# Block 2 of a fused attention and GeGLU kernel: two pairs of units in seven products, another order of units, earlier numerators and a later load of v

## The chip, the cores and the metric

The kernel runs on one core of one Trainium2 chip. The metric is the time of one execution on the device in microseconds (us). Three runs of the kernel before the change gave a median of 306.35 us (306.07 to 306.92).

## The reference

Inputs are q, k and v (batch 8, heads 8, sequence 576, head dimension 64) and three weight matrices. Attention is linear: no softmax over pairs of positions.

```python
def phi(x, c, s):                       # c, s: cosine and sine of pi/2 * position / 576
    r = np.maximum(x, 0.0)
    return np.concatenate([r * c, r * s], axis=-1)
kv = np.einsum('bhsf,bhsd->bhfd', k_p, v)        # k_p = phi(k), q_p = phi(q)
z = np.sum(k_p, axis=2)
num = np.einsum('bhsf,bhfd->bhsd', q_p, kv)
den = np.einsum('bhsf,bhf->bhs', q_p, z)[..., None] + 1e-06
x = (num / den)                          # then as 4608 tokens x 512
gelu = 0.5 * g * (1 + erf(g / sqrt(2)))  # g = x @ w_gate   (512 x 1536)
out = (gelu * (x @ w_val)) @ w_out       # 4608 x 512
```

## The kernel before

The work has two streams that are woven by hand. The attention goes by batch `b` (0 to 7, 576 tokens each). The feed-forward part goes by block `n` (0 to 8) of 512 tokens, so block 2 holds the last 128 tokens of batch 1 and 384 of batch 2, and block 3 the last 192 of batch 2 and the first 320 of batch 3. Each engine executes its instructions in the order in which the program issues them. TensorE is PE, VectorE is DVE, ScalarE is ACT, GpSimd is POOL, and SyncE (SP) issues most DMAs.

**Attention.** `load` brings q, k, v of a batch into staging (`st`, or `sm` and `fs` for some batches). The preps multiply the positive part by cosine (`c`) or sine (`s`), for one of nine groups of positions at a time; `prep_both` does q and k together, and `EARLY` lists by unit of block 2 which groups of batch 4 are prepared ("s0 c0": sine and cosine of group 0). There `early` puts sines on ACT, and cosines on POOL up to unit 8 and on ACT later. `cast_v` rounds v, `kv_unit` makes the product of k and v, and `turn_q` transposes q by two DMAs on SP. `nm_unit(b, t)` makes the numerators of 128 tokens: eight matmuls into PSUM banks 6 and 7, then on DVE a small add (`den`), a reciprocal (`rec`) and the division (`x_sb`, one of four buffers in turn, so that (3,2) takes that of (2,3) and (3,4) that of (3,0)). `turn_x(b, t)` transposes such a tile into `xT` by DMA on SP.

**Gate and value.** A unit is 128 of the 1536 columns of the gate and value weights, for one block. `gv_unit` (matmuls L431) runs four matmuls of 512 columns for the gate into one bank, a gelu on ACT (L440), four for the value into another bank, and a multiplication on DVE (L443) into the hidden tile `hT`. Block 2 of the kernel before makes all twelve units in this way, units 0 to 3 as two halves of 256 tokens each. Blocks 3 to 8 make most units two at a time, by `Pair`: seven products (`p1` to `p7`, L655) of four 256-column matmuls each stand for the eight that a plain two-by-two split needs. They need sums of weights (`ws`, `wx`), made in early blocks, and four sums of x, T1 to T4, made by `x_sum` on POOL (L635) in `fs`. Product 5 needs T1, product 6 T2, product 7 T3 and product 4 T4. Between the products ACT copies partial results (L674 copies product 1 from the pair's sum bank to its other bank, L678 product 5 to `fs`), and DVE adds (L682 after product 6, L695 after product 7) and multiplies (L696, L700). `step` writes out the order for one pair, with pieces of other work (`a`, `b`, `c`) between products. With `std` set it also makes one plain unit, with product 4 between its gate and its value.

**Output.** `o_step(n, jt)` does one or two of the fourteen products of the previous block's output (`product`, matmuls L548, six of 256 columns each, in banks 4 and 5). Copies (L566) and additions (L561) follow on ACT and DVE, and sums of hidden tiles (`h_sum`, L530) on DVE in block 2 and on POOL from block 3.

In the trace of before, block 2 runs on PE from 79 to 111 us. SP gives its DMAs eight completion semaphores in turn, so that an issue also waits for the landing of the DMA eight issues before it.

Of the kernel before, what the change touches and what calls it, by code (L numbers as in the profile page):

```python
# [10 lines left out]
BF16 = mybir.dt.bfloat16  # L11
# [5 lines left out]
def kernel(  # L17
# [20 lines left out]
    JT = J // 128  # L38
    NP = H // 2
    R = S // 64  # L40
    NB = B * S // 512
    NT = 5
    EPS = 1e-6
    BLK = 512
# [37 lines left out]
    fs = fast.tile([128, 5 * BLK], FP32)  # L82
# [138 lines left out]
    def turn_q(b):  # L221
        for i in range(2):
            nc.sync.dma_start_transpose(
                out=qt_tile(b)[:, i].rearrange("f m (j p) -> f (m j) p", p=64),
                in_=phi["q", b][64 * i:64 * i + 64].rearrange("p m j f -> p (m j f)"),
            )
# [83 lines left out]
    def nm_unit(b, t, b0=6):  # L310
        for h in range(H):
            nc.tensor.matmul(  # L312
                bank(b0 + h // 4)[:, (h % 4) * (D + 1):(h % 4 + 1) * (D + 1)],
                lhsT=q_cols(b, t, h),
                rhs=kv_sb[b][:, h // 2, h % 2, :],
                start=True,
                stop=True,
            )
        nm = ps[:, b0:b0 + 2, 0:4 * (D + 1)].rearrange("p g (h d) -> p g h d", h=4)
        den = attn2.tile([128, 2, 4], FP32, name="den")  # L320
        rec = attn2.tile([128, 2, 4], FP32, name="rec")
        x = xsp.tile([128, 2, 4, D], BF16, name="x_sb")
        nc.vector.tensor_scalar_add(den, nm[:, :, :, D], EPS)
        nc.vector.reciprocal(rec, den)
        nc.vector.tensor_tensor(  # L325
            x,
            nm[:, :, :, 0:D],
            rec[:, :, :, None].to_broadcast([128, 2, 4, D]),
            op=ALU.mult,
        )  # L330
        xs[b, t] = x.rearrange("p g h d -> p (g h d)")
# [44 lines left out]
    def turn_x(b, t):  # L376
        x = xs.pop((b, t))
        for blk, c, o, m in pieces(b, t):
            nc.sync.dma_start_transpose(
                out=xT_block(blk)[:, :, c:c + m], in_=x[o:o + m, :]  # L380
            )
# [13 lines left out]
    turn = [0]  # L395
# [25 lines left out]
    def gv_unit(n, jt, c0=0, w=BLK, to=None, between=None):  # L421
        xt = xT[n]
        js = slice(jt * 128, (jt + 1) * 128)
        if to is None:
            to = (0, 1) if turn[0] % 2 == 0 else (2, 3)
            turn[0] += 1
        if n not in hT:
            hT[n] = ffn.tile([128, JT, BLK], BF16, name="hT")
        for g, wt in ((0, wg_sb), (1, wv_sb)):
            for ct in range(CT):  # L430
                nc.tensor.matmul(  # L431
                    bank(to[g])[:, 0:w],
                    lhsT=wt[:, ct, js],
                    rhs=xt[:, ct, c0:c0 + w],
                    start=(ct == 0),
                    stop=(ct == CT - 1),
                )
            if g == 0:
                gel = ffn.tile([128, BLK], FP32, name="gel")
                nc.scalar.activation(gel[:, 0:w], bank(to[0])[:, 0:w], AF.Gelu)  # L440
                if between:
                    between()
        nc.vector.tensor_mul(  # L443
            hT[n][:, jt, c0:c0 + w], gel[:, 0:w], bank(to[1])[:, 0:w]
        )
# [57 lines left out]
    hs, rest = {}, [0]  # L503
# [119 lines left out]
    def x_sum(n, i, eng=nc.gpsimd):  # L623
        if n not in xb:
            xt = xT[n]
            own = fs[:, (n % 2) * 2 * BLK:(n % 2 + 1) * 2 * BLK].bitcast(BF16)
            xb[n] = {
                "B11": xt[:, 0:CP, 0:256], "B12": xt[:, 0:CP, 256:512],
                "B21": xt[:, CP:CT, 0:256], "B22": xt[:, CP:CT, 256:512],
                "T": own.rearrange("p (i c n) -> p i c n", i=4, c=CP),  # L630
            }
        b = xb[n]
        x, y = (("B12", "B11"), ("B22", "T1"), ("B22", "B12"), ("B21", "T2"))[i]
        b[f"T{i + 1}"] = b["T"][:, i]
        eng.tensor_tensor(b[f"T{i + 1}"], b[x], b[y], op=ALU.subtract)  # L635
# [98 lines left out]
    HALF = BLK // 2  # L734
# [151 lines left out]
    def js(a, b):  # L886
# [2 lines left out]
    LOADS = {  # L889
        (1, 4): [(3, "k")], (1, 9): [(3, "v", 0)], (1, 11): [(3, "v", 2)],  # L890
        (2, 0): [(4, "q", 0, 5), (4, "k", 0, 5)],
        (2, 2): [(4, "q", 5, R), (4, "k", 5, R), (4, "v")],
        (2, 9): [(5, "q", 0, 5), (5, "k", 0, 5)],
        (3, 1): [(5, "q", 5, R), (5, "k", 5, R), (5, "v")],
        (3, 9): [(6, "q", 0, 5), (6, "k", 0, 5)],
# [12 lines left out]
    MORE = {}  # L908
    for n in (3, 4, 5, 6):
        for i in range(4):  # L910
            MORE.setdefault((n - 1, 8 + i), []).append((n, i))
    for i, name in enumerate(("S1", "S3", "S2", "S4")):
        MORE.setdefault((6, i), []).append((name, WX, J))
    for i in range(4):
# [3 lines left out]
    def more(n, jt):  # L918
        for what in MORE.get((n, jt), ()):
            if len(what) == 3:  # L920
                w_sum(*what, eng=nc.gpsimd)
            else:
                x_sum(*what)
# [42 lines left out]
    def block1():  # L966
        b, n = 2, 1
        for jt in range(JT):
            i = jt - 9
            if i > 0:  # L970
                nm_unit(b, i, (4, 6, 4)[i])
                turn_x(b, i)
            if jt < 2:
                for i in range(2):
                    half, unit = divmod(2 * jt + i, 2)
                    x3 = lambda: turn_x_pe(1, 3, 5, dve_copy)
                    gv_unit(n, unit, half * HALF, HALF, between=x3 if jt == i == 0 else None)
                    j = JA + 2 * jt + i
                    prep("q", b, 1, (j,), eng=nc.scalar)
                    prep("q", b, 0, (j,))  # L980
            else:
                gv_unit(n, jt, between=(lambda: nm_unit(b, 0, 4)) if i == 0 else None)
            if i == 0:
                turn_x(b, 0)
            if jt % 3 == 1:
                flush()
            if jt == 2:
                prep("q", b, 0, (R - 1,))
                prep("q", b, 1, (R - 1,), eng=nc.scalar)
                turn_q(b)  # L990
                nm_unit(1, NT - 1)
            if jt == 5:
                turn_x(1, NT - 1)
            if jt == 6:
                kv_unit(b)
            if jt in (0, 1, 2, 7):
                wo_sum({0: "T3", 1: "T1", 2: "T2", 7: "T4"}[jt])
            if jt in SCALE:
                scale(*SCALE[jt])
            if jt in (3, 4):  # L1000
                cast_v(b, 2 * (jt - 3), 2 * (jt - 3) + 2, act_copy)
            if jt == 11:
                nm_unit(b, 3, 6)
            start_loads(n, jt)

    EARLY = {
        6: "s0 c0 s1 c1", 7: "s2 c2 s3", 8: "c3 s4", 9: "c4 s5", 10: "c5 s6", 11: "c6 s7",
        12: "c7 s8 c8",
    }

    def early(jt):
# [4 lines left out]
    def block2():  # L1016
        b, n = 3, 2
        o_step(n, 0)
        for jt in range(JT):
            if jt >= 4:  # L1020
                gv_unit(n, jt, to=(2, 6) if jt == JT - 1 else None)
            else:
                for i in range(2):
                    half, unit = divmod(2 * jt + i, 4)
                    gv_unit(n, unit, half * HALF, HALF)
                    if jt == i == 0:
                        nm_unit(2, 4)
                        turn_q(3)
            if 0 <= jt - 6 < NT:
                turn_x(b, jt - 6)  # L1030
            if 0 < jt < JT - 1:
                o_step(n, jt)
            if 0 <= jt - 5 < NT:
                nm_unit(b, jt - 5)
            if jt + JT in SCALE:
                scale(*SCALE[jt + JT])
            if jt in (1, 2):
                cast_v(b, 2 * jt - 2, 2 * jt, act_copy)
            if jt == 3:
                kv_unit(b)  # L1040
            early(jt)
            if jt == 1:
                turn_x(2, 3)
                turn_x(2, 4)
            start_loads(n, jt)
            if jt in (8, 9):
                m = 2 * (jt - 8)
                cast_v(4, m, m + 2, nc.gpsimd.tensor_copy)
            more(n, jt)

    turn[0] = 1
    block1()
    block2()

    PREPS = {
        2: "s0 c0", 4: "s1 c1", 5: "s2", "m10": "c2", 6: "s3 c3", 7: "s4 c4",
# [49 lines left out]
    def slot(n, jt):  # L1106
        o_step(*divmod(n * JT + jt - 1, JT))
        attention(n, jt)
        more(n, jt)
        if n == NB - 1 and jt in (9, 10):  # L1110
            h_sum(n, jt - 9, "S3", eng=nc.gpsimd)
        if n == NB - 1 and jt == 11:
            for name in ("S1", "S2", "S4"):
                h_sum(n, 0, name, 0, JH - 2, eng=nc.gpsimd)

    def slots(n, *jts):
        return [lambda jt=jt: slot(n, jt) for jt in jts]

    old, places = None, (0, 1, 2)
    for n in range(3, NB):  # L1120
        jt = 0
        for T in range(JT // 2):
# [3 lines left out]
            at, other, to = places  # L1126
# [60 lines left out]
```

## Time and profile before

| | |
|---|---|
| median of three runs | 306.35 us |
| the profiled execution | 305.74 us, its span 304.0 us |
| granted TensorE clock | 0.999 |
| busy, share of the span | PE 97%, DVE 75%, ACT 67%, POOL 55% |
| chain that ended last | PE 75%, DMA 8% |

PE is the row of matmuls and PEld that of weight loads, which lie beside the matmuls. In a timeline, a row gives start and duration (us), engine, line, operation, output and inputs, and how many; in brackets stands the idle time of the engine before it and what ended that. Rows of matmuls overlap their successors, since a matmul's end is counted when its last column leaves the array: what a group occupies is the distance from its start to the next group's start. In the chain of waits each row is the start, the length, and the engine or DMA that the end was waiting for at that moment.

### The profile page before, as it was taken

To read this page: it belongs to the slowest core of one execution; us is meant where nothing else is said; L and a number is where in the kernel's file an instruction comes from. 1 tells how busy PE (TensorE), PEld (TensorE's weight loads), DVE (VectorE), ACT (ScalarE), POOL (GpSimd) and SP (SyncE) were. 2 spreads that over 40 slices of the span, in tenths; PEclk is the share of its full clock that TensorE was granted. 3 is DMA by queue.
4 is the path that set the end of the run, shared out by engine and by line. 5 is a ranking of instruction groups with operands and counts; after the bars stand their busy time and mean duration, and the time that the engine had idled before them with its cause. 6 is when DMAs were issued, how large, how long until landed. Compare 5 with 4: busy or idle time off the path is not lost.

```text
span 304.0 us, 8032 instructions
## 1 busy us (share of the span) xinstructions
PE 294.7 (97%) x3089; PEld 228.8 (75%) x3107; DVE 226.7 (75%) x496; ACT 202.2 (67%) x399; POOL 165.9 (55%) x140
## 2 busy tenths in 40 slices
PE   7899999999999999999999999999999999999993
PEld 3574456745786668887888788888898988888882
DVE  5866995998986655779677967796679785766772
ACT  7865592997572787969686958694645556555630
POOL 6675450000000979976944694569935965397310
PEclk9999999999999999999999999999999999999999
DMA  7999999979999999997998899928824221303045
GB/s 269 258 174 218 338 293 390 309 162 224 183 169 231 320 239 170 207 298 215 130 238 251 215 135 226 277 31 136 139 55 71 53 51 30 71 0 73 2 87 121
DMA packets 73176, 53.68 MB, mean 177 GB/s; under 512 B 45393, under 2 KB 62545, under 8 KB 73137
## 3 DMA queue, kind: packets, MB, share of 16 engines
q1 hardware_dynamic: 63360, 41.17, 60.9%
q0 software_dynamic: 9696, 11.93, 17.1%
q8 instruction: 24, 0.39, 0.5%
q14 instruction: 16, 0.12, 0.2%
q10 hardware_dynamic: 80, 0.07, 0.1%
HBM read 37.75 MB, written 9.44 MB: 155 GB/s over the span
## 4 chain that ended last, share of the span: by engine, by line
PE 75%; DMA 8%; issue 5%; DVE 4%; POOL 3%; ACT 2%; SPq 1%; POOLq 0%; DVEq 0%; ACTq 0%
PE ps L655 32%; PE ps L548 19%; PE ps L431 14%; DMA st<-in_v_dram 5%; PE ps L464 3%; PE ps L271 3%; PE ps L312 2%; DMA wv_sb<-in_moe_w_val_dram 2%; DVE hT L443 2%; SPq L98 1%; POOL st L530 1%; DMA xT<-x_sb 1%; ACT phis L178 1%; PE ps L402 1%; POOL fs L635 1%
## 5 line engine op out<-in xcount | busy, mean ns | idle before, releaser
L530 POOL TENSOR_TENSOR sm<-hT 128x768 bf16<-128x768 bf16 x24 | 39.4, 1643 | 18.5 <-PE ps L655 8.0
L431 PE MATMUL ps<-xT,wg_sb 128*128 128x512 bf16 (+1 forms) x172 | 41.3, 349 | 0.6
L431 PE MATMUL ps<-xT,wv_sb 128*128 128x512 bf16 (+1 forms) x182 | 41.8, 351 | 0.1
L695 DVE TENSOR_TENSOR ps<-fs,ps 128x512 f32<-128x512 f32 x33 | 23.0, 696 | 24.7 <-PE ps L655 23.2
L655 PE MATMUL ps<-fs,ws 128*128 128x256 bf16 x288 | 40.8, 273 | 0.1
L655 PEld LDWEIGHTS <-ws 128*128 128x128 bf16 x384 | 36.5, 98 | 5.1 <-ACT ps L674 0.3
L655 PE MATMUL ps<-xT,wg_sb 128*128 128x256 bf16 x264 | 39.6, 272 | 0.0
L194 POOL TENSOR_SCALAR phis<-st,cos_t 128x512 bf16<-128x512 f32 x4 | 8.2, 2067 | 52.4 <-DMA st<-in_k_dram 52.4
L443 DVE TENSOR_TENSOR hT<-gel,ps 128x512 bf16<-128x512 f32 (+1 forms) x46 | 28.0, 613 | 11.5 <-PE ps L431 8.8
L548 PEld LDWEIGHTS <-sm 128*128 128x128 bf16 x336 | 32.3, 98 | 4.5
L440 ACT ACTIVATE gel<-ps 128x512 f32<-128x512 f32 (+1 forms) x46 | 24.6, 542 | 15.7 <-PE ps L431 14.5
L687 ACT ACTIVATE gel<-ps 128x512 f32<-128x512 f32 x33 | 19.6, 594 | 18.3 <-PE ps L655 18.3
L548 PEld LDWEIGHTS <-hT 128*128 128x128 bf16 x288 | 27.9, 98 | 4.0 <-issue 0.2
L561 DVE TENSOR_TENSOR o_sb<-sm,ps 128x256 f32<-128x256 f32 x56 | 23.3, 416 | 10.1 <-ACT sm L566 8.9
L678 ACT COPY fs<-ps 128x512 f32<-128x512 f32 x33 | 19.4, 587 | 16.2 <-DVE ps L695 15.3
L431 PEld LDWEIGHTS <-wv_sb 128*128 128x128 bf16 x184 | 17.9, 98 | 15.2 <-issue 0.3
L655 PEld LDWEIGHTS <-wg_sb 128*128 128x128 bf16 x264 | 25.8, 98 | 4.7
L325 DVE TENSOR_TENSOR x_sb<-ps,rec 128x512 bf16<-128x512 f32 x38 | 26.3, 691 | 1.3
L192 ACT ACTIVATE phis<-st,sin_t 128x512 bf16<-128x512 f32 x36 | 25.6, 718 | 0.0
L530 POOL TENSOR_TENSOR sm<-hT,sm 128x768 bf16<-128x768 bf16 x12 | 19.7, 1645 | 10.8 <-PE ps L548 10.8
L431 PEld LDWEIGHTS <-wg_sb 128*128 128x128 bf16 x184 | 17.0, 98 | 11.4
L696 DVE TENSOR_TENSOR hT<-gel,ps 128x512 bf16<-128x512 f32 x33 | 22.7, 687 | 3.2
(134 smaller groups left out, 636.0 us busy)
## 6 DMA issues: line engine op xcount, KB each, us to landing
out_dram<-o_sb SPq DMA_DIRECT2D x69, 128.0 KB, 3.0
st<-in_v_dram SPq DMA_DIRECT2D x10, 576.0 KB, 7.5
st<-in_q_dram SPq DMA_DIRECT2D x5, 640.0 KB, 5.4
st<-in_q_dram SPq DMA_DIRECT2D x5, 512.0 KB, 5.6
st<-in_k_dram SPq DMA_DIRECT2D x4, 640.0 KB, 5.9
st<-in_k_dram SPq DMA_DIRECT2D x4, 576.0 KB, 4.6
st<-in_q_dram POOLq DMA_DIRECT2D x4, 576.0 KB, 12.1
st<-in_k_dram SPq DMA_DIRECT2D x4, 512.0 KB, 5.4
```

The source lines that it names most:

```text
L192: nc.scalar.activation(o, i, AF.Relu, scale=tab[:, j:j + 1])
L325: nc.vector.tensor_tensor(x, nm[:, :, :, 0:D], rec[:, :, :, None].to_broadcast([128, 2, 4, D]), op=ALU.mult,)
L431: nc.tensor.matmul(bank(to[g])[:, 0:w], lhsT=wt[:, ct, js], rhs=xt[:, ct, c0:c0 + w], start=(ct == 0), stop=(ct == CT - 1),)
L440: nc.scalar.activation(gel[:, 0:w], bank(to[0])[:, 0:w], AF.Gelu)
L443: nc.vector.tensor_mul(hT[n][:, jt, c0:c0 + w], gel[:, 0:w], bank(to[1])[:, 0:w])
L530: eng.tensor_tensor(a[name][:, j0:j1], a[x][:, j0:j1], a[y][:, j0:j1], op=op)
L548: nc.tensor.matmul(at, lhsT=hs.setdefault(key, h_parts(n, p))[a][:, j], rhs=ts[b][:, j], start=(j == 0 and i in ((1, 2, 4, 5), (1, 4, 5))[ ...
L561: nc.vector.tensor_tensor(o, got[key, k], x, op=op)
L655: nc.tensor.matmul(to[:, 256 * half:256 * half + 256], lhsT=w_part(a, j * 128, (j + 1) * 128)[:, ct], rhs=xb[self.n][b][:, ct], start=(hal ...
L687: nc.scalar.activation(self.gel0, self.other, AF.Gelu)
L695: nc.vector.tensor_tensor(bank(val), self.m5, self.sum, op=ALU.add)
L696: nc.vector.tensor_tensor(self.h(1), both(gel1), both(bank(val)), op=ALU.mult)
```

## The change

Block 2 takes units 8 to 11 first, as halves, then unit 4 whole, then units 0 and 1 as a pair with unit 5 plain inside it, units 2 and 3 as a pair with unit 6 inside it, and unit 7 at the end. The sums of x for block 2 are made on POOL at unit 2, and those for blocks 2 and 3 change halves of `fs`. The work that was put behind each unit is now the function `rest`, in which the numerators of batch 3 and their transposes stand one unit sooner. All four sums for block 3 are issued at unit 8, and the casts of v of batch 4 follow them at units 9 and 10. v of batch 4 is loaded at unit 7, where it was at unit 2. The preps of batch 4 are spread differently, and the last unit uses banks 0 and 6 where it was 2 and 6.

```diff
     def x_sum(n, i, eng=nc.gpsimd):
-            own = fs[:, (n % 2) * 2 * BLK:(n % 2 + 1) * 2 * BLK].bitcast(BF16)
+            own = fs[:, (1 - n % 2) * 2 * BLK:(2 - n % 2) * 2 * BLK].bitcast(BF16)
...
-        (2, 2): [(4, "q", 5, R), (4, "k", 5, R), (4, "v")],
+        (2, 2): [(4, "q", 5, R), (4, "k", 5, R)],
+        (2, 7): [(4, "v")],
...
-            MORE.setdefault((n - 1, 8 + i), []).append((n, i))
+            MORE.setdefault((n - 1, 8 + i * (n > 3)), []).append((n, i))
...
     EARLY = {
-        6: "s0 c0 s1 c1", 7: "s2 c2 s3", 8: "c3 s4", 9: "c4 s5", 10: "c5 s6", 11: "c6 s7",
-        12: "c7 s8 c8",
+        7: "c0 c1 c2 c3 s0 s1 s2", 8: "s3 s4", 9: "c4", 10: "s5 c5 s6", 11: "c6 s7 c7",
+        12: "s8 c8",
     }
...
     def block2():
         b, n = 3, 2
         o_step(n, 0)
-        for jt in range(JT):
-            if jt >= 4:
-                gv_unit(n, jt, to=(2, 6) if jt == JT - 1 else None)
-            else:
-                for i in range(2):
-                    half, unit = divmod(2 * jt + i, 4)
-                    gv_unit(n, unit, half * HALF, HALF)
-                    if jt == i == 0:
-                        nm_unit(2, 4)
-                        turn_q(3)
-            if 0 <= jt - 6 < NT:
-                turn_x(b, jt - 6)
+
+        def rest(jt):
+            if 0 <= jt - 5 < NT:
+                turn_x(b, jt - 5)
             if 0 < jt < JT - 1:
                 o_step(n, jt)
-            if 0 <= jt - 5 < NT:
-                nm_unit(b, jt - 5)
+            if 0 <= jt - 4 < NT:
+                nm_unit(b, jt - 4)
...
             start_loads(n, jt)
-            if jt in (8, 9):
-                m = 2 * (jt - 8)
+            if jt == 2:
+                for i in range(4):
+                    x_sum(n, i)
+            more(n, jt)
+            if jt in (9, 10):
+                m = 2 * (jt - 9)
                 cast_v(4, m, m + 2, nc.gpsimd.tensor_copy)
-            more(n, jt)
+
+        def rests(*jts):
+            return [lambda jt=jt: rest(jt) for jt in jts]
+
+        turn[0] = 1
+        for jt in range(4):
+            for i in range(2):
+                half, unit = divmod(2 * jt + i, 4)
+                gv_unit(n, unit + 8, half * HALF, HALF)
+                if jt == i == 0:
+                    nm_unit(2, 4)
+                    turn_q(3)
+            rest(jt)
+        gv_unit(n, 4, to=(2, 6))
+        rest(4)
+        step(Pair(n, 0, 0, 2, range(5, 8)), None, *rests(5, 6, 7), std=5, to=1)
+        step(Pair(n, 1, 2, 0, range(8, 11)), None, *rests(8, 9, 10), std=6, to=1)
+        gv_unit(n, 7, to=(0, 6))
+        rest(11)
```

More of the change, by code (lines that the diff above doesn't have):

```diff
@@ L1045, in block2 @@
             start_loads(n, jt)
-            if jt in (8, 9):
-                m = 2 * (jt - 8)
-                cast_v(4, m, m + 2, nc.gpsimd.tensor_copy)
-            more(n, jt)
-    turn[0] = 1
-    block1()
-    block2()
+            if jt == 2:
[4 more added lines that the diff above has]
+                m = 2 * (jt - 9)
+                cast_v(4, m, m + 2, nc.gpsimd.tensor_copy)
+        def rests(*jts):
[15 more added lines that the diff above has]
+        rest(11)
     PREPS = {
@@ L1117, in slots @@
         return [lambda jt=jt: slot(n, jt) for jt in jts]
+    turn[0] = 1
+    block1()
+    block2()
     old, places = None, (0, 1, 2)
```

## The prediction

> **What bounds the kernel now.** I read the page first, then the chain of waits from 85 to 116 us, then the timelines of TensorE (PE), VectorE (DVE), ScalarE (ACT), GpSimd (POOL) and SyncE (SP) over block 2, 79 to 113 us. Page, part 1:
>
> ```profile
> PE 294.7 (97%) x3089; PEld 228.8 (75%) x3107; DVE 226.7 (75%) x496; ACT 202.2 (67%) x399; POOL 165.9 (55%) x140
> ```
>
> PE is the bound, and in block 2 its matmuls follow each other without a hole but one. So whatever PE no longer runs is gained, and every new wait of PE is lost one for one. The chain of waits (start, us, what) tells of that hole:
>
> ```profile
> 96.60 0.83 SPq L98
> 97.48 9.34 DMA st<-in_v_dram
> 106.83 2.76 DMA xT<-x_sb
> 109.61 1.15 POOL fs L635
> 110.76 1.09 POOL vx L209
> 111.86 1.12 POOL fs L635
> 113.02 1.03 PE ps L655 x8
> ```
>
> v of batch 4 lands, then the x tiles behind it, then POOL makes T1, casts, makes T2, and product 6 of block 3 starts at 113.02. The PE timeline has the hole and, earlier, unit 4 with what follows:
>
> ```profile
> 91.78 1.03 PE L431 MATMUL ps<-xT,wv_sb 128*128 128x512 bf16 x4
> 92.65 0.82 PE L548 MATMUL ps<-T,hT 128*128 128x256 bf16 x6
> 93.30 1.03 PE L431 MATMUL ps<-xT,wg_sb 128*128 128x512 bf16 x4
> 112.14 0.82 PE L548 MATMUL ps<-wo_sb,sm 128*128 128x256 bf16 x6
> 113.02 0.60 PE L655 MATMUL ps<-fs,ws 128*128 128x256 bf16 x4
> ```
>
> Six matmuls of 256 occupy PE 0.66 (92.65 to 93.30), so PE was free at 112.80 and stood 0.22. DVE and ACT, same stretch:
>
> ```profile
> 92.92 0.69 DVE L443 TENSOR_TENSOR hT<-gel,ps 128x512 bf16<-128x512 f32 x1 [1.28 <-PE ps L431]
> 107.84 0.16 DVE L323 TENSOR_SCALAR den<-ps 128x8 f32<-128x8 f32 x1
> 108.03 0.20 DVE L324 RECIPROCAL rec<-den 128x8 f32<-128x8 f32 x1
> 108.27 0.69 DVE L325 TENSOR_TENSOR x_sb<-ps,rec 128x512 bf16<-128x512 f32 x1
> 110.60 0.60 ACT L440 ACTIVATE gel<-ps 128x512 f32<-128x512 f32 x1 [0.20 <-PE ps L431]
> 111.09 0.71 ACT L192 ACTIVATE phis<-st,cos_t 128x512 bf16<-128x512 f32 x1
> 111.71 0.71 ACT L192 ACTIVATE phis<-st,sin_t 128x512 bf16<-128x512 f32 x1
> 112.32 0.58 ACT L674 COPY ps<-ps 128x512 f32<-128x512 f32 x1
> ```
>
> Each engine works in program order. ACT starts some 0.20 after PE is free, DVE 0.27 (92.65 to 92.92), PE some 0.05 after the DVE or ACT result it needs (T2 ended 112.98, PE 113.02). ACT's copy of product 1 ended 112.90, so without T2's wait product 6 still stands about 0.13 there.
>
> **The products.** A unit is eight 512-column matmuls, four in 0.865 (91.78 to 92.65): two units 3.46. A pair is seven products of four 256-column matmuls, 0.4375 each (116.57 to 117.01 in block 3): 3.06. Gain 0.40 a pair, **0.80** for two. The Trainium skill, "TensorE: Matmul & The Clock Gate", Back-to-back issue gap, speaks against that: sustained it gives about 131 ns for a 512-column matmul and 81 for 128, so, put between them (an estimate), about 98 for 256, and a pair would take 2.73 against 2.10 and two pairs cost 1.3. This trace has 216 and 109, and I go by it.
>
> **Parts that I cost at nothing.** Units 8 to 11 as halves: the same rows; hT of block 2 is read first at 113.89. Sums of block 2's x: four on POOL at 1.11 each, behind the second cast of v 3 (ACT, 88.03 to 89.17): done 93.7. POOL is idle until 98.06; the last is read by p4 at about 101; if that cover went, p5 (94.4) and p6 (95.8) would wait for T1 (90.4) and T2 (91.5), which have over 4 us to spare. DVE's sums of hidden tiles (0.55 each) would lie beside them, which no row of before shows; bounds 0 to 0.5 on DVE, I take 0, as POOL and DVE durations elsewhere (block 3) are alike with and without overlap. The Trainium skill, "GPSIMD Engine Reference", has GpSimd's SBUF interfaces shared with VectorE where a DVE instruction has two SBUF inputs; no row here overlaps the two. v of batch 4 (two issues of 0.5 to 0.8 on SP) goes behind the tiles of (3,2) and two stores; I expect landing near 109 and 110. POOL: c0 to c3 end 106.2, four x sums to 110.7, casts to 113.0. kv of batch 4 wants them at about 116.5: 3 us of cover. On SP the move takes two issues from ahead of all the tiles of batch 3: before, a tile's issue at 106.83 stood until v had landed at 106.81. Behind v on SP there are now the tiles of (3,3) and (3,4) and the first loads of batch 5, which need prep c4 (ACT, 107.7; before 108.0): no one waits for those before block 3. The single units 5 and 6 use one bank for gate and value: the gelu ends 0.80 after the gate, while PE has a product, a numerator and p4, over 1.1. New fs half: no time. Last unit into banks 0 and 6: product 1 of block 3 needs bank 0, read by the gelu that ends 0.20 + 0.60 = 0.80 after the gate; the value matmuls take 0.865. Hidden by 0.02 at worst, a wait of 0.05 otherwise.
>
> **Numerators a unit sooner: new waits of PE.** Times in the clock of before.
> (a) nm(3,0) follows unit 4 and product 4, at 93.30. It writes bank 6, where unit 4's value now lies (to=(2, 6)), and DVE reads that until 92.92 + 0.69 = 93.61. PE goes on at 93.66: **0.36**. Its other inputs are there (turned q landed 92.95 by the trace's completion updates, kv copies by 91.7).
> (b) nm(3,1), after p1, p5 and a product (0.44 + 0.44 + 0.66), wants bank 6 at 95.45. DVE runs o_sb, a hidden sum (to 94.40), den, rec and x of nm(3,0) to 95.5: **0.10**.
> (c) x(3,2) reuses the buffer of x(2,3), whose transposed tile landed at 99.98. Before, DVE wrote x(3,2) at 102.52 and saw nothing; now it would at 99.55 and stands to 100.03. Behind it on DVE: the add of product 7, which p4 waits for. x to 100.7, add to 101.35. PE: nm(3,3) **0.08** (bank 6), and p4, wanted at 101.03, **0.35**. If that tile landed 1.5 sooner, both are 0; nothing ahead of it in the queue is changed, so I take 0.43.
> (d) Second pair. nm(3,4) stands right ahead of p6. DVE after PE's end of nm: 0.27, den 0.20, rec 0.24, x 0.61, then p6's add, 0.69, and 0.05 back: 2.06. p3 overwrites the add's bank and needs it; PE has p6, p2 and one product till then, 0.44 + 0.44 + 0.66 = 1.54: **0.53**. In the first pair the same place has two products and a numerator (2.0 after p6), no wait.
> (e) p4 of the second pair: add of product 7 waits for gelu behind prep c4 on ACT: **0.05**.
>
> **ACT's preps.** Now c6, s7, c7 follow the last unit's gelu, before c6, s7: three steps of 0.62 ahead of product 1's copy. From the gate's end: 0.20 + gelu 0.49 + 1.85 + copy 0.58 + 0.04 = 3.16. PE till product 6: value 0.865, p1 and p5 0.875, product 0.66 = 2.40. Wait **0.76**, in place of 0.22; T2 (108.6) is no longer late. What follows is c8, s8: ACT had slack there (0.93 idle at 116.67).
>
> **Sum.** 0.36 + 0.10 + 0.43 + 0.53 + 0.05 + 0.76 = 2.23 of waits, less the old 0.22, less 0.80: +1.21 us. The profiled execution took 305.74 (span 304.0, 1.74 around it) and would take 306.95; it stood 0.61 under the median of the runs, 306.35. Median forecast: 306.35 + 1.2, about **307.5**, 0.4% slower. Block 3 and later are bound by PE and shift as a whole.
>
> **Rivals.**
> 1. Faster: the waits are covered and the products count. Full gain 0.80 + 0.22: 305.3. For it: PE has one hole in 35 us, and pairs in block 3 run without (a wait of 0.08 in the first). Against: there products of the pair before lie between; here (a) and the ACT row are arithmetic on in-order queues. It decides at waits under 0.1 in sum. Chance 0.07.
> 2. About even: (c) goes and DVE and ACT are 0.1 to 0.2 quicker to respond at (d) and product 6: +0.3 to +0.9, centre 306.9. Nothing against it but the rows' repeatability. Chance 0.25.
> 3. The x buffers bite: x(3,4) reuses the buffer of x(3,0). Before, that tile landed 107.99 behind v of batch 4; v took 103.26 to 106.24 of the queue, so I place it at 105.0, and DVE wants the buffer at 105.19. If moving v frees nothing, DVE stands to 108 and p3 waits 3.4 instead of 0.53: +4.1, 310.4; half of that, +2.5, 308.9. It decides from 105.2 on, one for one. Chance 0.12.
> 4. The change does not bring the x tiles sooner: T2 stays late. That lies under the 0.76 of ACT until T2 passes 114.2 (before 112.98). Cost 0; part of 3.
>
> **How the numbers follow.** Forecast case 0.56, own range 307.0 to 308.2 (bounds: (e), the 0.1 and the DVE sharing above, 0 to 0.5, each way). About 0.3% (0.92 us: 305.43 to 307.27) is what a measurement of this kernel can tell from no change. Slower by more: most of the forecast case (0.49) and case 3, 0.61. Faster: case 1 with little else, 0.07. Within: 0.32. The range 306.2 to 308.9 leaves out case 1 and the far half of case 3 and some of the rest, 0.2 in all.
>
> **What would show it.** Right: nm(3,0) starting 0.05 after DVE's L443 of unit 4; DVE's x at the third numerator ended by an xT transfer; a hole of about 0.5 before p3 of the second pair; 0.7 to 0.8 before product 6 of block 3 with ACT L674 as its releaser; and product groups of 0.44. Wrong: no holes of PE in block 2, or a hole above 1 us at p3 of the second pair (case 3), or one at kv of batch 4 (v too late), or matmul groups of the pairs longer than 0.44.

## The result, and the profile after

The changed kernel takes 307.57 us (median of 22 runs, 306.76 to 308.58), against 306.58 us for the kernel before in the same rounds (22 runs, 305.08 to 307.17). The ratio is 1.004 with a 95% interval of 1.0028 to 1.0053: slower by 0.9 to 1.6 us. All ratios here are of fast runs: two of the twelve runs of the last kernel below were slow ones, 309.95 and 310.18 us, some 4 above the other ten, for which no trace shows a cause, and they stand outside its ratio.

The profiled execution of the changed kernel took 308.40 us (span 306.6). That is 2.7 more than the profiled one of before, but part of it has nothing to do with the change: the work ahead of block 2 ended anywhere from 78.5 to 80.3 us in the profiles of this case, with the same program there. So the text compares a **stretch**: from the first output product of block 2 to the first product of k and v of batch 4, early in block 3. It is 36.27 us before (36.22 in a second execution) and 37.97 after, a loss of 1.70. From there to the last matmul both take the same, 183.25 and 183.26 us. All of the loss is in the stretch. Where an expectation reckons to product 6 of block 3, which starts 2.28 sooner, that is 33.99 before and 35.68 after.

From the page of the changed kernel (engine, busy time, share of the span, instructions):

```profile
PE 295.4 (96%) x3131; PEld 231.0 (75%) x3131; DVE 230.6 (75%) x500; ACT 203.9 (66%) x403; POOL 169.2 (55%) x144
```

PE's busy time is no lower than before and its share fell: time was lost to holes. The timeline of PE over the places that the prediction named:

```profile
93.59 0.82 PE L548 MATMUL ps<-T,hT 128*128 128x256 bf16 x6
94.60 0.42 PE L312 MATMUL ps<-kv_sb,qT 128*128 128x65 bf16 x8 [0.19 <-DVE hT L443]
...
95.73 0.82 PE L548 MATMUL ps<-wo_sb,sm 128*128 128x256 bf16 x6
97.04 0.42 PE L312 MATMUL ps<-kv_sb,qT 128*128 128x65 bf16 x8 [0.50 <-DVE x_sb L325]
97.30 0.60 PE L655 MATMUL ps<-fs,ws 128*128 128x256 bf16 x4
97.73 0.60 PE L655 MATMUL ps<-xT,wg_sb 128*128 128x256 bf16 x4
...
107.76 0.60 PE L655 MATMUL ps<-xT,ws 128*128 128x256 bf16 x4 [0.29 <-DVE ps L682]
```

Six matmuls of 256 columns occupy 0.655, so nm(3,0) stood 94.60 − 93.59 − 0.655 = 0.36 and nm(3,1) 97.04 − 95.73 − 0.655 = 0.66 (the idle time in brackets is less by some 0.16, since a matmul's end is counted later). A group of a pair takes 97.73 − 97.30 = 0.43. The timelines of DVE and of POOL ahead of nm(3,1):

```profile
91.43 0.55 DVE L530 TENSOR_TENSOR sm<-hT 128x768 bf16<-128x768 bf16 x1
92.01 1.39 DVE L530 TENSOR_TENSOR sm<-sm,hT 128x768 bf16<-128x768 bf16 x1
93.86 0.69 DVE L443 TENSOR_TENSOR hT<-gel,ps 128x512 bf16<-128x512 f32 x1 [0.45 <-PE ps L431]
...
94.80 1.16 DVE L530 TENSOR_TENSOR sm<-hT 128x768 bf16<-128x768 bf16 x1
```

```profile
91.43 1.56 POOL L635 TENSOR_TENSOR fs<-xT,fs 128x512 bf16<-128x512 bf16 x1
92.95 1.46 POOL L635 TENSOR_TENSOR fs<-xT 128x512 bf16<-128x512 bf16 x1
94.38 1.15 POOL L635 TENSOR_TENSOR fs<-xT,fs 128x512 bf16<-128x512 bf16 x1
```

Hidden sums on DVE that take 0.55 alone took 1.39 and 1.16, and two of the sums of x on POOL took 1.56 and 1.46 instead of 1.15. In order of their ends: DVE 91.98, POOL 92.99, DVE 93.40, POOL 94.41, POOL 95.53, DVE 95.96. It reads as one of them standing until the other's instruction is through.

The chain of waits at the end of the block (start, us, what), where before the x tiles and T2 stood:

```profile
113.17 1.93 ACT phis L192 x3
115.11 0.49 ACT ps L674
115.60 0.05 issue
115.65 1.05 PE ps L655 x8
```

Behind the last unit's gelu stand three preps, the copy of product 1, and product 6 at 115.65. PE had been free since 114.86, a hole of 0.79.

The holes of PE in the stretch, but for those of 0.10 that both kernels have at products of k and v. A hole is there where the distance of two matmuls is more than the first one's length (0.216 for 512 columns, 0.109 for 256, 0.033 for 65):

| hole ahead of | predicted | measured |
|---|---|---|
| (a) nm(3,0) | 0.36 | 0.36 |
| (b) nm(3,1) | 0.10 | 0.66 |
| (c) nm(3,3) and p4, first pair | 0.08 + 0.35 | 0 + 0.28 |
| (d) p3, second pair | 0.53 | 0.46 |
| (e) p4, second pair | 0.05 | 0.13 |
| first product of block 3 | 0 to 0.05 | 0.03 |
| product 6 of block 3 | 0.76 | 0.79 |
| sum | 2.23 | 2.71 |

2.71 less the old hole of 0.23 less 0.80 for the pairs is +1.68, and the stretch grew by 1.70. It is a little more than the top of the timed interval, 1.62; nothing here explains the rest.

### The profile page after: what moved, and what is told of

Its sections match the earlier page's. It is cut to its first block, busy times and chain, and to the rows that moved or that the text cites. A ratio compares the mean times of both kernels' runs of the same rounds, so it can differ in the third digit from the quotient of the medians.

```text
span 306.6 us, 8114 instructions
## 1 busy us (share of the span) xinstructions
PE 295.4 (96%) x3131; PEld 231.0 (75%) x3131; DVE 230.6 (75%) x500; ACT 203.9 (66%) x403; POOL 169.2 (55%) x144
## 4 chain that ended last, share of the span: by engine, by line
PE 78%; DVE 7%; issue 5%; DMA 5%; ACT 2%; POOL 1%; SPq 0%; POOLq 0%; DVEq 0%; ACTq 0%
PE ps L655 33%; PE ps L548 19%; PE ps L431 15%; PE ps L464 3%; PE ps L312 3%; DMA st<-in_v_dram 3%; PE ps L271 2%; DMA wv_sb<-in_moe_w_val_dram 2%; DVE hT L443 2%; DVE phis L180 1%; POOL st L530 1%; PE ps L402 1%; DVE x_sb L325 1%; PE ps L234 1%; ACT phis L192 1%
## 5 line engine op out<-in xcount | busy, mean ns | idle before, releaser
L635 POOL TENSOR_TENSOR fs<-xT 128x512 bf16<-128x512 bf16 x14 | 16.5, 1176 | 58.9 <-ACT vx L209 45.4
L655 PE MATMUL ps<-fs,ws 128*128 128x256 bf16 x312 | 44.4, 273 | 0.6 <-ACT ps L674 0.6
L655 PEld LDWEIGHTS <-ws 128*128 128x128 bf16 x416 | 39.4, 98 | 6.5 <-ACT ps L674 0.9
L695 DVE TENSOR_TENSOR ps<-fs,ps 128x512 f32<-128x512 f32 x35 | 24.3, 695 | 25.4 <-PE ps L655 23.2
L655 PE MATMUL ps<-xT,wg_sb 128*128 128x256 bf16 x280 | 42.0, 272 | 0.0
L431 PE MATMUL ps<-xT,wg_sb 128*128 128x512 bf16 (+1 forms) x168 | 38.0, 349 | 0.0
L431 PE MATMUL ps<-xT,wv_sb 128*128 128x512 bf16 (+1 forms) x168 | 38.0, 349 | 0.0
L687 ACT ACTIVATE gel<-ps 128x512 f32<-128x512 f32 x35 | 20.8, 593 | 20.4 <-PE ps L655 18.6
L561 DVE TENSOR_TENSOR o_sb<-sm,ps 128x256 f32<-128x256 f32 x56 | 23.4, 417 | 10.5 <-ACT sm L566 9.2
L655 PEld LDWEIGHTS <-wg_sb 128*128 128x128 bf16 x280 | 27.3, 98 | 5.1 <-issue 0.2
L443 DVE TENSOR_TENSOR hT<-gel,ps 128x512 bf16<-128x512 f32 (+1 forms) x42 | 25.3, 606 | 7.5 <-PE ps L431 5.2
L440 ACT ACTIVATE gel<-ps 128x512 f32<-128x512 f32 (+1 forms) x42 | 22.2, 536 | 12.6 <-PE ps L431 11.5
L691 ACT ACTIVATE gel<-ps 128x512 f32<-128x512 f32 x35 | 20.9, 598 | 8.2 <-PE ps L655 6.9
```

The lines of the kernel that those rows point to most:

```text
L431: nc.tensor.matmul(bank(to[g])[:, 0:w], lhsT=wt[:, ct, js], rhs=xt[:, ct, c0:c0 + w], start=(ct == 0), stop=(ct == CT - 1),)
L443: nc.vector.tensor_mul(hT[n][:, jt, c0:c0 + w], gel[:, 0:w], bank(to[1])[:, 0:w])
L561: nc.vector.tensor_tensor(o, got[key, k], x, op=op)
L655: nc.tensor.matmul(to[:, 256 * half:256 * half + 256], lhsT=w_part(a, j * 128, (j + 1) * 128)[:, ct], rhs=xb[self.n][b][:, ct], start=(hal ...
L691: nc.scalar.activation(gel1, bank(MIX), AF.Gelu)
L695: nc.vector.tensor_tensor(bank(val), self.m5, self.sum, op=ALU.add)
```

## The experiments

Each is an edit of the changed kernel, but for one. Where nothing else is said, a figure is the length of the stretch or of one hole in one profiled execution.

**The changed kernel again.** No edit.

> The changed kernel again, for the spread of its own rows. The stretch from the first output product of block 2 to product 6 of block 3's first pair was 33.99 us before (79.03 to 113.02) and 35.68 after (79.97 to 115.65). If the order on each engine decides, the stretch comes out within 0.15 of 35.68 again, with holes of PE near 0.36, 0.66, 0.28, 0.46, 0.13 and 0.79. Rival: the holes hang on when transfers land and vary by run; then the stretch moves by 0.3 or more.

The stretch is 37.97 again, and every hole repeats within 0.01, though this execution reached block 2 0.59 us earlier. The holes come from the order of work on the engines, so differences of a tenth can be read.

**The kernel before again.** No edit.

> The kernel before again, for the spread of its rows: stretch 33.99 within 0.1, one hole of 0.23 before product 6 of block 3. If it comes out 0.3 or more off, single profiles do not carry differences of tenths.

The stretch is 36.22 (33.93 to product 6) and the hole at product 6 0.17 (36.27 and 0.23 in the first profile). That hole hung on the landing of x tiles, and it moves by some hundredths.

**One prep behind product 1's copy.**

```diff
-        11: "c6 s7 c7",
-        12: "s8 c8",
+        11: "c6 s7",
+        12: "c7 s8 c8",
```

> Prep c7 goes back from unit 11 to slot 12, so that two steps instead of three stand on ScalarE ahead of product 1's copy. Queue theory: the hole before product 6 of block 3 falls from 0.79 by one step, 0.62, to 0.15 to 0.25; the stretch falls from 35.68 to about 35.05. Rival: T2 or the x tiles hold product 6, and the hole stays near 0.8.

The timeline of PE in this kernel:

```profile
114.06 0.82 PE L548 MATMUL ps<-wo_sb,sm 128*128 128x256 bf16 x6
114.91 0.61 PE L655 MATMUL ps<-fs,ws 128*128 128x256 bf16 x4
```

Product 6 starts 0.85 after the product ahead of it, where it was 1.45. The hole fell from 0.79 to 0.19 and the stretch from 37.97 to 37.36 (35.07 to product 6): a prep of 0.62 on ACT was worth 0.60 of the stretch. What is left is what two preps leave: the copy L674 ended at 114.85, so ACT still decides there, not T2.

**No sums of x in block 2.** This kernel leaves the four sums for block 2 out, and the products read single parts of x.

```diff
     def x_sum(n, i, eng=nc.gpsimd):
+        if eng is None:
+            b[f"T{i + 1}"] = b[x if i < 2 else "B22"]
+            return
...
-                    x_sum(n, i)
+                    x_sum(n, i, eng=None)
```

> The four sums of x of block 2 are left out on GpSimd (the products of its two pairs read single parts of x in their place). Theory: GpSimd's sums and VectorE's sums of hidden tiles slow each other. Then the hidden sums at the end of unit 3 and at unit 4 take 0.55 again where they took up to 1.16, the hole before nm(3,1) falls from 0.66 to about 0.10, p4 of the first pair waits a little more (0.28 to about 0.4, since the buffer of x(2,3) then decides), and the stretch is about 35.2. Rival: the hidden sums were long for another reason (a write of TensorE or a DMA); then they stay above 1 and the stretch stays at 35.7.

Its timelines of DVE and of PE:

```profile
90.57 0.56 DVE L530 TENSOR_TENSOR sm<-sm,hT 128x768 bf16<-128x768 bf16 x1
...
93.35 0.55 DVE L530 TENSOR_TENSOR sm<-hT 128x768 bf16<-128x768 bf16 x1
```

```profile
94.28 0.82 PE L548 MATMUL ps<-wo_sb,sm 128*128 128x256 bf16 x6
94.99 0.42 PE L312 MATMUL ps<-kv_sb,qT 128*128 128x65 bf16 x8
```

The same two hidden sums that took 1.39 and 1.16 take 0.56 and 0.55, and nm(3,1) follows its product after 0.71: the hole is 0.06. So (b) is POOL's sums of x lengthening DVE's sums. The stretch fell 0.57, to 37.40 (35.10 to product 6). The hole ahead of p3 of the second pair grew from 0.46 to 0.61, since PE now comes to it sooner and the tile of (3,0) less so (DVE's x stood 0.19 for it). The hole ahead of p4 of the first pair stayed, 0.30 where 0.28 was; the 0.4 expected from the buffer of x(2,3) did not come.

**Unit 4's value into another bank.**

```diff
-        gv_unit(n, 4, to=(2, 6))
+        gv_unit(n, 4, to=(2, 1))
```

> Unit 4 puts its value into bank 1 instead of 6, so nm(3,0) has no bank to wait for. Queue theory: the hole of 0.36 before nm(3,0) goes, but VectorE is not sooner with x(3,0), so nm(3,1) waits by as much more: 0.66 becomes 1.0, and the stretch stays within 0.1 of 35.68. Rival: each hole is a cost of its own; then the stretch falls by 0.36 to 35.3.

The timeline of PE:

```profile
94.49 0.42 PE L312 MATMUL ps<-kv_sb,qT 128*128 128x65 bf16 x8
...
97.29 0.42 PE L312 MATMUL ps<-kv_sb,qT 128*128 128x65 bf16 x8 [0.85 <-DVE x_sb L325]
```

Hole (a) is gone and (b) grew from 0.66 to 1.01: the 0.36 came back whole at the next numerator. The stretch is 38.04, no shorter (the hole ahead of p4 of the first pair grew by 0.07). What sets nm(3,1) is DVE's queue, which does not move when PE starts nm(3,0) sooner. That each hole has a price of its own fell here.

**Numerators at units 5 to 9, as before.**

```diff
-            if 0 <= jt - 4 < NT:
-                nm_unit(b, jt - 4)
+            t = {5: 0, 6: 1, 7: 2, 8: 3, 9: 4}.get(jt)
+            if t is not None:
+                nm_unit(b, t)
```

(The transposes `turn_x` of these tiles stand a unit later likewise.)

> The numerators of batch 3 and their transposes stand where they stood before the change (units 5 to 9); all else as after. Queue theory: the holes before nm(3,0) (0.36) and nm(3,1) (0.66) go, p3 and p4 of the second pair wait about 0.25 each, product 6 of block 3 still 0.79 for ScalarE; the x tile of (3,2) lands some 2.5 later, so that GpSimd's sums and casts end later and kv of batch 4 waits about 0.5. Stretch to product 6: 34.6 in place of 35.68; to kv 37.45 in place of 37.97. Rival: the unit sooner is what pays for the early sums T1 to T4; then product 6 waits longer than 0.79 without it and the stretch does not fall.

The view of waits from 79 to 118 us (engine and line, waited for: us in total, times, longest):

```profile
PE ps L655 <- ACT ps L674: 0.6, 1, 0.6
PE ps L271 <- POOL vx L209: 0.6, 2, 0.3
```

Holes (a) and (b) are gone. To product 6 of block 3 it is 34.69, against 35.68 in the changed kernel: 0.99, about (a) and (b) together (p3 and p4 of the second pair have 0.20 and 0.39, in the sum as much as the 0.46 and 0.13 before). But the tiles land later, POOL's sums and casts with them, and products of k and v wait for the casts. Of the 0.99 the first of them gives back 0.36 (the stretch is 37.34), and what follows takes 0.50 longer (183.78 us, where 183.28 is usual). In this order the earlier numerators buy time for POOL, for about as much as they cost.

**Plain units in place of the pairs.** Order, numerators, loads and preps as in the changed kernel; units 0 to 3 are made singly and block 2 has no sums of x.

```diff
-            if jt == 2:
-                for i in range(4):
-                    x_sum(n, i)
...
-        gv_unit(n, 4, to=(2, 6))
-        rest(4)
-        step(Pair(n, 0, 0, 2, range(5, 8)), None, *rests(5, 6, 7), std=5, to=1)
-        step(Pair(n, 1, 2, 0, range(8, 11)), None, *rests(8, 9, 10), std=6, to=1)
+        for jt, unit in enumerate((4, 0, 1, 5, 2, 3, 6), 4):
+            gv_unit(n, unit, to=((2, 6), (0, 1), (2, 3))[0 if jt == 4 else 1 + jt % 2])
+            rest(jt)
```

> Units 0 to 3 plain again in place of the two pairs, in the order 4, 0, 1, 5, 2, 3, 6, 7, no sums of x for block 2; numerators, load of v and preps as after. Theory: PE runs 0.80 more, but the holes inside the pairs (0.28, 0.46, 0.13) and the one from shared access (0.66) go; left are 0.36 before nm(3,0) and about 0.79 before product 6. Stretch 33.99 + 0.36 + 0.56 = 34.9, 0.8 under after. Rival: the holes come with the earlier numerators, pairs or not, and the plain units only add 0.8: stretch 36.4.

The timeline of PE at nm(3,1):

```profile
97.02 0.82 PE L548 MATMUL ps<-wo_sb,sm 128*128 128x256 bf16 x6
97.67 0.42 PE L312 MATMUL ps<-kv_sb,qT 128*128 128x65 bf16 x8
```

The numerators follow their product after 0.65. The stretch is 37.37 (35.09 to product 6), which is 0.60 shorter than with the pairs. Holes (b) to (e) are gone but for 0.12 ahead of nm(3,3); (a) and the one at product 6 are as they were. The pairs run 0.80 less on PE and bring 0.66 + 0.28 + 0.46 + 0.13 − 0.12 = 1.41 of holes with them.

**v of batch 4 loaded at unit 2, as before.**

```diff
-        (2, 2): [(4, "q", 5, R), (4, "k", 5, R)],
-        (2, 7): [(4, "v")],
+        (2, 2): [(4, "q", 5, R), (4, "k", 5, R), (4, "v")],
```

> v of batch 4 loaded at unit 2 again, ahead of the x tiles; all else as after. Theory: the tile of (3,0) lands some 2.5 later, VectorE waits for its buffer at x(3,4), and p3 of the second pair waits 2.5 to 3.0 instead of 0.46: stretch about 38. Rival: tiles and v do not hold each other up; stretch stays at 35.68.

Its timelines of DVE and of PE, and two rows of the windows view (stretch, its length, then for PE, PEld, DVE, ACT and POOL busy time and instructions, granted TensorE clock, DMA share, GB/s):

```profile
106.80 0.69 DVE L325 TENSOR_TENSOR x_sb<-ps,rec 128x512 bf16<-128x512 f32 x1 [1.85 <-DMA xT<-x_sb]
```

```profile
105.22 0.82 PE L548 MATMUL ps<-T,sm 128*128 128x256 bf16 x6
108.15 0.60 PE L655 MATMUL ps<-xT,ws 128*128 128x256 bf16 x4 [2.11 <-DVE ps L682]
```

```profile
105.00:108.50 3.50, 1.39 (x14) 1.09 (x12) 1.62 (x3) 2.59 (x5) 1.27 (x2) 1.00 1.12 277
108.50:112.30 3.80, 3.58 (x17) 2.19 (x16) 1.38 (x2) 1.81 (x4) 3.72 (x5) 0.55 0.55 124
```

x(3,4) takes the buffer of x(3,0), whose tile lands behind v; DVE stands 1.85 for it and p3 of the second pair starts 2.27 late. The stretch is 41.34 (39.05 to product 6, where about 38 was expected), or 3.37 longer than in the changed kernel. The hole is 1.81 of that. The rest has the second cause that no theory had: behind the hole the granted clock was 0.55 in the mean of 3.8 us (by narrower windows 0.50 from about 108.9 to 112.3, and 1.00 again from there), and matmuls took twice their time.

**A better placing.** Four edits together: numerators and transposes at units 5 to 9, as in the experiment of that name; only one prep ahead of product 1's copy; one hidden sum of DVE from unit 6 to unit 8; and the casts of v between the second and third sum of x on POOL.

```diff
-        2: {0: "1", 1: "2", 2: "34", 3: "56", 4: "7", 6: "8"},
+        2: {0: "1", 1: "2", 2: "34", 3: "56", 4: "7", 8: "8"},
...
-        11: "c6 s7 c7",
-        12: "s8 c8",
+        11: "c6",
+        12: "s7 c7 s8 c8",
...
+            if jt == 8:
+                for i in range(4):
+                    x_sum(3, i)
+                    if i == 1:
+                        for m in (0, 2):
+                            cast_v(4, m, m + 2, nc.gpsimd.tensor_copy)
```

> Pairs kept, with the causes of the holes taken out: numerators at units 5 to 9 as before, prep order 11 c6 and 12 s7 c7 s8 c8, the hidden sum of unit 6 at unit 8, and the casts of v of batch 4 between the second and the third sum of x of block 3. Queue theory: from the numerators-late run (37.34 to kv) minus the 0.79 before product 6, the 0.28 before p4 of the first pair and the 0.36 before kv: about 35.9 to kv, 0.3 to 0.4 under before (36.22 and 36.27); time 0.1% to 0.2% under before. Rival: each hole filled opens another of its size, since VectorE and ScalarE are as full as PE in the pairs; then the stretch stays above 36.8 and the time above before.

**The same, and one prep sooner.** Sine of group 3 of batch 4 goes from unit 8 to unit 7, ahead of the second pair's gelus on ACT.

```diff
-        7: "c0 c1 c2 c3 s0 s1 s2", 8: "s3 s4",
+        7: "c0 c1 c2 c3 s0 s1 s2 s3", 8: "s4",
```

> The same with sine s3 of batch 4 at unit 7 instead of 8, so that ScalarE reaches the gelus of the second pair one step (0.62) sooner. Queue theory: p4 of the second pair waits for the addition of product 7, which waits for the gelu of product 3 or for VectorE's x(3,4); if the gelu decides, its hole (0.39 in the numerators-late run) falls by 0.2 to 0.4; if VectorE decides, nothing changes against the run beside it. Time within 0.1% of that run either way.

The first has 35.69 us of stretch, with two holes of note: 0.20 ahead of p3 and 0.22 ahead of p4 of the second pair. Behind the stretch 183.60 us follow, where before has 183.25, so 0.23 is left of the 0.58. The second has 35.47 and only the first of these holes. In both the add L695 that p4 needs follows DVE's x(3,4) at once; what brought it forward was ACT's queue, since DVE's add L561 ahead of x(3,4) stood 0.54 for ACT's copy L566 in the first kernel and 0.20 in the second. The timeline of PE of the second at p3 and at product 6 of block 3:

```profile
105.46 0.42 PE L312 MATMUL ps<-kv_sb,qT 128*128 128x65 bf16 x8
105.92 0.60 PE L655 MATMUL ps<-xT,ws 128*128 128x256 bf16 x4
...
112.24 0.82 PE L548 MATMUL ps<-wo_sb,sm 128*128 128x256 bf16 x6
112.90 0.60 PE L655 MATMUL ps<-fs,ws 128*128 128x256 bf16 x4
```

p3 follows eight matmuls of 65 columns (0.26) after 0.46, a hole of 0.20; product 6 follows at once (0.66). The stretch is 0.80 shorter than before: the pairs' whole gain. Behind it 183.39 us follow (183.25 before); the 0.14 more is a hole between products of k and v. Timed in five rounds, with 23 runs of the kernel before at 306.36: the first takes 306.37 (12 runs), ratio 0.9999 with an interval of 0.9984 to 1.0013, no difference, where 0.1% to 0.2% was expected; the second 306.03 (12 runs), ratio 0.9981, of ten of them, with an interval of 0.9967 to 0.9994. In these ten it is faster than the kernel before by 0.2 to 1.0 us, where the profiles give 0.66; over all twelve the mean is 306.56, no lower than the 306.40 of before. The two intervals overlap, so what the last prep is worth by itself is read from the profiles alone.

## Why the prediction was right, and where it was not

**Sign and size.** Forecast +1.2 us, 307.5; measured 307.57, and by the ratio +1.2 (0.9 to 1.6). In the traces the loss is 1.70, so the sum was 0.49 short. That the timed time lies on the forecast is in part luck: (b) was 0.56 short and (c) and (d) 0.22 over, the kernel before stood at 306.58 in these rounds where the forecast set out from 306.35, and the timed runs show less of a loss than the traces.

**The pairs' gain, 0.80.** Right: groups of 0.43 to 0.44, as in block 3. The estimate from the page's issue gap, which would have had the pairs cost 1.3, does not hold here.

**(a) 0.36, and product 6 of block 3, 0.76.** Right in size and mechanism, 0.36 and 0.79, each shown by taking its cause away. Yet the price of (a) was not its own: in this kernel, without it, nm(3,1) waits as much longer.

**(b) 0.10: the term that was mis-sized, 0.66.** The step that failed is the one "I take 0", for DVE's hidden sums beside POOL's sums of x, with 0.5 as the upper bound; the hole grew by more than that bound. The excess was 0.84 on one and 0.61 on the other, 1.45 in all. The first lay under an idle time of DVE, which shrank from 1.28 (without the sums of x) to 0.45; the second stood ahead of den, rec and x of nm(3,0), on the path, and is 0.60 of the stretch at that place. The argument for 0 was drawn from rows of block 3, where DVE's work beside POOL's sums reads one operand from PSUM; those rows could not show it. The sentence that no row of before overlaps such work missed one, where a hidden sum of DVE lies on the seam of two preps of POOL:

```profile
98.06 8.22 POOL L194 TENSOR_SCALAR phis<-st,cos_t 128x512 bf16<-128x512 f32 x4 [52.44 <-DMA st<-in_k_dram]
99.92 0.55 DVE L530 TENSOR_TENSOR sm<-hT,sm 128x768 bf16<-128x768 bf16 x1
```

The sum took its 0.55, but POOL's four preps took 8.22, where they take 7.91 in the changed kernel and in the second execution of before, in which the sum lies inside one prep. The Trainium skill, "GPSIMD Engine Reference", Specifications, has the SBUF interfaces shared with VectorE, with contention when a DVE instruction has two SBUF inputs. These traces agree for POOL's sums of x: the DVE sums with two SBUF inputs were lengthened, 0.55 to 1.39 and 1.16, while L443 at 90.42, which reads PSUM, was not.

**(c) 0.43.** Measured 0.28, by another chain:

```profile
100.09 0.42 DVE L561 TENSOR_TENSOR o_sb<-sm,ps 128x256 f32<-128x256 f32 x1 [0.85 <-ACT sm L566]
100.42 0.55 DVE L530 TENSOR_TENSOR sm<-hT,sm 128x768 bf16<-128x768 bf16 x1
...
101.93 0.69 DVE L695 TENSOR_TENSOR ps<-fs,ps 128x512 f32<-128x512 f32 x1
```

The buffer of x(2,3) held nobody: its tile landed at 101.13, and DVE came to x(3,2) at 101.32. DVE was late since its add L561 stood 0.85 for ACT's copy L566 of an output product (to 100.06), and a hidden sum (0.47) followed before den, rec, x and the add L695 that p4 needs. The prediction followed DVE from the numerators and missed that wait for ACT, which the trace of before has too (0.96, ahead of L561 at 99.58). It is there without POOL's sums (0.84, hole 0.30). With the numerators a unit later and nothing else changed the hole stays at 0.28; in the better placings, where that hidden sum stands later too, DVE waits 0.79 and 0.78 for ACT and the hole is gone. So it was the hidden sum that filled DVE's time there: the other edits of the first of these come behind that place.

**(d) 0.53 and (e) 0.05.** Measured 0.46 and 0.13, by the chains named: DVE's L682 is the releaser of p3, and the add L695 ahead of p4 waits 0.69 for ACT's gelu L691.

**Rivals.** The first fell; the best placing comes nearest to its condition of waits under 0.1, with 0.23 of holes. The second, +0.3 to +0.9, touches the timed interval only at its lower end; what it names, (c) and (d), was smaller by 0.22 together. The third's mechanism is real, as the early v shows, but the move of v frees the tile: in the changed kernel that of (3,0) landed at 105.48, some 0.9 before DVE wanted it. (In the clock of before that is 104.54. The prediction placed it at 105.0 by an end of v at 106.24, which no row of a DMA gives; v landed at 106.81, and with that the same working gives 104.4.) The fourth's condition did not come about, since T2 ended at 109.47, where it was 112.98 before; that ACT and not T2 decides at product 6 is as forecast.

**The whole, taken apart.** The kernel with plain units loses 1.10 against before: (a) 0.36, product 6 0.78 − 0.23, and 0.18 in two smaller holes. The pairs in their place lose 0.60 more. Together 1.70.

## What to carry to other kernels

A saving on the engine that bounds a kernel counts only where the engines that feed it have slack at that very place: here 0.80 us of products came with 1.41 us of holes, and moving one hidden sum, three preps and two casts brought the 0.80 of the stretch back, with the numerators where they had been. Before costing an operation on another engine at nothing, look for a row in which the very same kinds of operands overlap; if there is none, take the whole length of the other instruction as the upper bound (here 1.15, of which 0.84 and 0.61 came). Holes that share a queue are not added or removed one by one: remove the first, and see whether the second grows by as much.

## What the runs showed of the hardware

**DVE and POOL.** A DVE sum of two SBUF operands (128x768, bf16) and a POOL sum (128x512, bf16) at the same time lengthen each other: 0.55 to 1.39 and 1.16, and 1.15 to 1.56 and 1.46, about as if they took turns. That does not go for all work of POOL: inside a prep of POOL (L194, one operand of 128x512, f32, 1.99) the same DVE sum took 0.55 in the changed kernel (at 100.42) and 0.73 in the first better placing (at 103.33, 0.36 into the prep).

**The clock.** Holes of up to 1.01 us in block 2 left the granted clock at 1.00. One of 2.27 us was followed by 3.4 us at 0.50, which cost some 1.5 us more than the hole itself. It was not the only one: near 11 us, far ahead of the stretch, four more profiles (one prep behind product 1's copy, unit 4's value into another bank, plain units, and the last kernel) have 3.41 us at 0.50. In the 3.41 us ahead of each of these five, PE was busy for 1.30 to 1.72 us. Where it was busy for 2.10 of as long a time (8.85 to 12.26 us in the second profile of before, 8.99 to 12.40 in the first better placing) the clock stayed at 1.00. The Trainium skill, "TensorE: Matmul & The Clock Gate", What's actually happening, has the clock halved after an idle window of about 3.4 us and back after as long a busy one. The second agrees with the 3.4 us here; the first does not, as PE had run for more than a third of that time in each of the five. Where between 1.72 and 2.10 the limit lies, and how the time is cut into windows, is open.
